# One recurrent-attention and MLP kernel: coefficients as one row spread by a product, filler transposes on TensorE, a fourth plain weight pair, and a new order table

## Chip, cores, metric

The kernel runs on one core of a Trainium2 chip. The metric is device time in microseconds (us) of one execution; smaller is better. Times of several runs are given by their median.

## What is computed

A gated linear attention over 4 x 8 sequences of 768 tokens with head size 48, and a two-layer MLP over the 3072 tokens with a rational function between its layers:

```
for t in range(S):                                  # B, H, S, D = 4, 8, 768, 48
    state = alpha[:, :, t, :, None] * state + k[:, :, t] outer v[:, :, t]
    y[:, :, t] = q[:, :, t] @ state
x = y as 3072 x 384
h = x @ w_in                                        # 384 x 2048
P = a[0] + a[1]*h + a[2]*h**2 + a[3]*h**3           # a: 4 numbers, b: 2 numbers
Q = 1 + |b[0]|*|h| + |b[1]|*h**2
out = (P / (Q + 1e-6)) @ w_out                      # 2048 x 384
```

The weights come as 64-bit floats.

## The kernel before

**Attention.** The sequences are cut into 24 chunks of 128 tokens, g = 0 to 23, with all 8 heads in one chunk. Per chunk, alpha, k and q are brought to a layout with tokens along the free axis: for the first two segments (four chunks) by TensorE transposes of loaded tiles (`turn_nat`, L515, steps `tn`) and ACT copies (L534, steps `cp`), later by DVE. Two scans on DVE give the running products from both sides (`suffix` L552, `prefix` L564, steps `suf`, `pre`); k and q are multiplied by them (L573, L576). Then TensorE transposes k (`kt`, L627), makes the scores (`s`, L594), adds to the state (`vk`, L664) and makes the chunk's y (`am`, L682). ACT and DVE copy scores out of PSUM (`se`, L615, L617) and half of q into place (`qc`, L604), GpSimd (POOL) masks them (L621). ACT writes y as x (`xh`, L712).

**MLP.** A job of layer one and two is either *wide* or *plain*. A wide job is one block of 128 hidden columns for 512 tokens: x, the weights and the rational function's result are each split into a high and a low half of a faster number format, and three products replace one (`in`: nine products of 512 columns, L792; `oh` and `ol`: nine, L811, or L805 for the last 512 tokens). A plain job is a weight pair j (256 hidden columns) for 256 tokens m, in full 32-bit floats (`plain_in` L765, `plain_out` L778; in the first jobs `in` is cut into two halves of 128 tokens). A plain product leaves two records in the trace. Plain jobs need only the whole x and the joined weights, no halves. The first `JP` = 3 pairs are plain for the first 512 tokens: jobs u = 0 to 5; the wide jobs follow, 96 jobs in all.

Between the layers each job runs through ACT (L853, L857, L860, L897), DVE (L864, L871, L874, L916) and, if wide, the split into halves (L924 or L926, L930).

**Weights.** A pair of each layer is loaded as 64-bit words (`w`, 768 KB) and made a 32-bit float: a scale step (`abs`, L358), a shift (`low`, L366), a sign step (`sign`, L370 on ACT or L372 on DVE) and `join` (L386). Pairs that are used plain are kept joined, copied by DMA later (`bring`) and split then (`hi`, `lo`); the others are split at once.

**Coefficients.** `load_coef` reads the 4 + 2 coefficients with two DMAs that repeat them over 128 partitions. Small DVE operations work out what the activations need (`unit_of`, `root_of`, `shift_of`, `sign_of`, `fits`).

**Order.** Every piece of work is a step with its engine and the steps that it comes after. A table of numbers (`ORDER`) holds the order in which all steps are written out, and with it each engine's own order; a bit in it chooses between two engines for steps that name an alternative. Each engine works its list strictly in order; loads are issued on the SP queue. At the start TensorE turns an identity matrix over 14 times (`warm`, L508) as soon as GpSimd has made it.

## Time and profile before

| | us |
|---|---|
| median of 3 runs | 511.21 (510.99 to 514.34) |
| the profiled execution | 509.78 |
| its span, from first to last instruction | 508.1 |
| TensorE busy | 489.1 (96%) |
| DVE busy | 439.3 (86%) |
| ACT busy | 400.3 (79%) |
| POOL busy | 274.3 (54%) |

By the chain that ended last, TensorE has 79% of the span and ACT 11%. In 40 slices of 12.7 us the TensorE digits are 7778899 for the first seven and 9 from then on to the last but one. The granted clock digit is 8 in the third and the fourth slice and 9 in all others.

### The profile page before, as it was taken

To read this page: it belongs to the slowest core of one execution; us is meant where nothing else is said; L and a number is where in the kernel's file an instruction comes from. 1 tells how busy PE (TensorE), PEld (TensorE's weight loads), DVE (VectorE), ACT (ScalarE), POOL (GpSimd) and SP (SyncE) were. 2 spreads that over 40 slices of the span, in tenths; PEclk is the share of its full clock that TensorE was granted. 3 is DMA by queue.
4 is the path that set the end of the run, shared out by engine and by line. 5 is a ranking of instruction groups with operands and counts; after the bars stand their busy time and mean duration, and the time that the engine had idled before them with its cause. 6 is when DMAs were issued, how large, how long until landed. Compare 5 with 4: busy or idle time off the path is not lost.

```text
span 508.1 us, 13259 instructions
## 1 busy us (share of the span) xinstructions
PE 489.1 (96%) x5062; PEld 411.1 (81%) x5062; DVE 439.3 (86%) x696; ACT 400.3 (79%) x726; POOL 274.3 (54%) x330
## 2 busy tenths in 40 slices
PE   7778899999999999999999999999999999999995
PEld 6668788787788888888888888888888888898994
DVE  4998999998998999889989989799888887877673
ACT  2898999999887778877797877788878676877572
POOL 2336567789977545647665455753646553321410
PEclk9988999999999999999999999999999999999999
DMA  7999784745643344645543545536544300321001
GB/s 199 266 280 279 193 233 96 178 99 128 154 111 86 85 92 103 106 115 117 114 97 81 122 92 114 120 82 125 98 104 79 64 22 1 57 32 17 1 0 66
DMA packets 144595, 55.98 MB, mean 110 GB/s; under 512 B 133520, under 2 KB 137104, under 8 KB 144528
## 3 DMA queue, kind: packets, MB, share of 16 engines
q1 hardware_dynamic: 143952, 54.70, 46.8%
q8 instruction: 41, 0.67, 0.6%
q10 hardware_dynamic: 576, 0.40, 0.2%
q14 instruction: 26, 0.21, 0.1%
HBM read 47.98 MB, written 4.72 MB: 104 GB/s over the span
## 4 chain that ended last, share of the span: by engine, by line
PE 79%; ACT 11%; DMA 4%; DVE 2%; issue 2%; POOL 1%; SPq 1%; ACTq 0%; DVEq 0%; POOLq 0%
PE ps L792 33%; PE ps L811 29%; PE ps L805 6%; PE ps L682 4%; PE ps L594 2%; PE ps L664 2%; ACT wi_words L370 1%; DMA wo_words<-in_moe_w_out_dram 1%; PE ps L627 1%; DMA wi_words<-in_moe_w_in_dram 1%; ACT t L860 1%; DMA coef<-in_moe_b_dram 1%; ACT qm L857 1%; ACT qm L853 1%; ACT tqk L615 1%
## 5 line engine op out<-in xcount | busy, mean ns | idle before, releaser
L792 PE MATMUL ps<-x,wi 128*128 128x512 f32 x810 | 201.8, 392 | 0.0
L792 PEld LDWEIGHTS ps<-x,wi 128*128 128x128 f32 x810 | 151.2, 188 | 31.2 <-DVE t L916 0.4
L811 PE MATMUL ps<-gh_gl,wo 128*128 128x512 f32 x666 | 167.7, 393 | 0.1
L811 PEld LDWEIGHTS ps<-gh_gl,wo 128*128 128x128 f32 x666 | 123.5, 188 | 26.5 <-POOL gh_gl L930 0.5
L930 POOL TENSOR_TENSOR gh_gl<-t,gh_gl 128x512 fp32r<-128x512 f32 x72 | 93.2, 1296 | 74.6 <-PE ps L811 20.6
L864 DVE SCALAR_TENSOR_TENSOR t<-t,mini,ps 128x512 f32<-128x512 f32 x96 | 70.8, 739 | 20.5 <-ACT t L860 14.5
L860 ACT ACTIVATE t<-ps,mini 128x512 f32<-128x512 f32 x96 | 65.7, 684 | 23.0 <-PE ps L792 10.7
L871 DVE SCALAR_TENSOR_TENSOR t<-t,mini,ps 128x512 f32<-128x512 f32 x96 | 70.6, 736 | 14.6 <-ACT ps L897 13.9
L853 ACT ACTIVATE qm<-ps 128x512 f32<-128x512 f32 x96 | 56.8, 594 | 22.4 <-PE ps L792 16.6
L897 ACT ACTIVATE ps<-qm 128x512 f32<-128x512 f32 x96 | 57.4, 601 | 21.2 <-DVE t L864 20.0
L857 ACT ACTIVATE qm<-qm,mini 128x512 f32<-128x512 f32 x96 | 69.3, 722 | 1.1
L926 POOL CAST gh_gl<-t 128x512 fp32r<-128x512 f32 x55 | 33.5, 612 | 62.8 <-DVE t L916 33.5
L916 DVE SCALAR_TENSOR_TENSOR t<-ps,t 128x512 f32<-128x512 f32 x96 | 65.7, 685 | 1.9
L874 DVE SCALAR_TENSOR_TENSOR ps<-qm,ps 128x512 f32<-128x512 f32 x96 | 65.9, 687 | 0.0
L621 POOL TENSOR_SCALAR_AFFINE_SELECT tqk<-tqk 64x512 f32<-64x512 f32 x48 | 31.5, 655 | 23.7 <-DVE tqk L617 11.4
L573 POOL TENSOR_TENSOR tqk<-tqk,tg 128x512 f32<-128x512 f32 x23 | 29.6, 1289 | 13.6 <-DVE wo_words L366 7.3
L805 PE MATMUL ps<-wo,gh_gl 128*128 128x384 f32 x180 | 34.1, 336 | 0.0
L805 PEld LDWEIGHTS ps<-wo,gh_gl 128*128 128x128 f32 x180 | 31.8, 188 | 1.3
L564 DVE TENSOR_TENSOR_SCAN fp<-ta,ps 128x528 f32<-128x528 f32 x24 | 29.9, 1244 | 1.4 <-ACT tqk L615 0.5
L552 DVE TENSOR_TENSOR_SCAN tg<-ta,ps 128x528 f32<-128x528 f32 x24 | 29.8, 1246 | 1.1 <-ACT qm L853 0.8
L576 POOL TENSOR_TENSOR tqk<-tqk,fp 128x512 f32<-128x512 f32 x19 | 24.6, 1295 | 7.2 <-DVE fp L564 4.0
L924 ACT ACTIVATE gh_gl<-t 128x512 fp32r<-128x512 f32 x35 | 21.9, 626 | 8.3 <-DVE t L916 8.2
(137 smaller groups left out, 619.4 us busy)
## 6 DMA issues: line engine op xcount, KB each, us to landing
raw_a<-in_alpha_dram SPq DMA_DIRECT2D x160, 48.0 KB, 2.1
wi_words<-in_moe_w_in_dram SPq DMA_DIRECT2D x8, 768.0 KB, 6.5
wo_words<-in_moe_w_out_dram SPq DMA_DIRECT2D x8, 768.0 KB, 6.0
sv<-in_v_dram SPq DMA_DIRECT2D x48, 96.0 KB, 2.8
wr<-in_alpha_dram SPq DMA_DIRECT2D x18, 256.0 KB, 3.0
raw_odd<-in_q_dram SPq DMA_DIRECT2D x80, 48.0 KB, 2.3
raw_qk<-in_k_dram SPq DMA_DIRECT2D x80, 48.0 KB, 2.2
raw_qk<-in_q_dram SPq DMA_DIRECT2D x80, 48.0 KB, 2.2
```

What stands on the lines that cost most here:

```text
L792: nc.tensor.matmul(h_of(u), w(key)[:, kt * FU + f % FU, :], x[:, kt, xp, :], start=(n == 0), stop=(n == len(todo) - 1),)
L805: nc.tensor.matmul(bank(T_BANKS[tt], DM), g[:, tt * P : (tt + 1) * P], w(("o", f // FU))[:, f % FU, :], start=(f == 0 and first_w), stop=( ...
L811: nc.tensor.matmul(bank(O_BANKS[dt]), w(("o", f // FU))[:, f % FU, dt * P : (dt + 1) * P], g, start=(f == 0 and first_w), stop=(f == NF - ...
L853: nc.scalar.activation(buf(s, "qm", u), h_of(u), AF.Abs)
L857: nc.scalar.activation(t, t, AF.Square, bias=shift[:, 1:2], scale=rq_reg)
L860: nc.scalar.activation(buf(s, "t1", u), h_of(u), AF.Square, bias=shift[:, 0:1], scale=rp_reg)
L864: nc.vector.scalar_tensor_tensor(t, t, rest, h_of(u), op0=ALU.add, op1=ALU.mult)
L871: nc.vector.scalar_tensor_tensor(t, t, part_of[:, 0:1], h_of(u), op0=ALU.add, op1=ALU.mult)
L874: nc.vector.scalar_tensor_tensor(h_of(u), buf(s, "qm", u), SMALL, h_of(u), op0=ALU.add, op1=ALU.mult)
L897: nc.scalar.add_instruction(mybir.InstActivation(name=nc.get_next_instruction_name(), engine=nc.scalar.engine, func=AF.Reciprocal, ins=[nc ...
L916: nc.vector.scalar_tensor_tensor(t, h_of(u), 2.0, t, op0=ALU.subtract, op1=ALU.mult, reverse0=True)
L930: eng.tensor_tensor(buf(s, "gl", u).rearrange("p a b -> p (a b)"), buf(s, "t1", u), gh, op=ALU.subtract)
```

## The change

- The coefficients are loaded into one partition (two DMAs of one row each). A DVE memset writes a row of 128 ones (`set_ones`), a TensorE product of that row with the coefficients puts them on all 128 partitions in PSUM (`coef_mm`), and a DVE copy brings them back (`coef_all`). The steps that use them come after the copy.
- Ten groups of four transposes of the identity into bank 7 (`fill`). Three may come from the point at which that bank's first user has been copied, seven after its second; the first `plain_out` comes after all of them.
- `JP` = 4: four plain pairs, jobs u = 0 to 7 (four with the first 256 tokens, four with the next), and two wide jobs fewer.
- A new order table.

```diff
--- before.py
+++ after.py
@@ -75,63 +75,64 @@
 
 
 ORDER = [
-    'c-jrt1Dhqv4nWaLDoItwwr$(CZQC}^^qHRS9^1BU+qP}n_ult@#QxR>6T`$b35+q(O=J_r#4`yE8*9{vnP|{VGLy|>v&@i*',
...
+    'c-jq>V}mBl4h1{iNjh2Ewr$(CZQHx=vokwd+qP}nwr$(E_ZOTmRdv7^V~sP34H`1>%oG#fL^E+sEEC;KGgHk5lhDL5QB7=<',
...
 ]
 
 
@@ -148,6 +149,7 @@
 }
 NNAT = 2
 WARM = 14
+FILL = (3, 7)
 WB = 2
 GB = 3
 NSC = 1
@@ -159,7 +161,7 @@
 NV = 2
 NTG = 2
 RB = 2
-JP = 3
+JP = 4
 HALF = 3
 Y_FROM = 8
 Y_AT = (4, 8, 12, 15)
@@ -236,8 +238,17 @@
     b0, b1 = bab[:, 0:1], bab[:, 1:2]
 
     def load_coef():
-        nc.scalar.dma_start(coef[:, 0:4], ca.unsqueeze(0).to_broadcast([P, 4]))
-        nc.scalar.dma_start(coef[:, 4:6], cb.unsqueeze(0).to_broadcast([P, 2]))
+        nc.scalar.dma_start(coef[0:1, 0:4], ca.unsqueeze(0))
+        nc.scalar.dma_start(coef[0:1, 4:6], cb.unsqueeze(0))
+
+    def set_ones():
+        nc.vector.memset(fp[0][0:1, 0:P], 1.0)
+
+    def coef_mm():
+        nc.tensor.matmul(bank(2)[:, P : P + 6], fp[0][0:1, 0:P], coef[0:1, :], start=True, stop=True)
+
+    def coef_all():
+        nc.vector.tensor_copy(coef, bank(2)[:, P : P + 6])
 
     a3_reg = nc.scalar.alloc_register("a3")
     b1_reg = nc.scalar.alloc_register("b1")
@@ -506,6 +517,10 @@
     def warm():
         for n in range(WARM):
             nc.tensor.transpose(bank(2, P), ident, ident)
+
+    def fill():
+        for n in range(4):
+            nc.tensor.transpose(bank(7, P), ident, ident)
 
     def turn_nat(m, nm, par):
         for a in range(NPAIR):
@@ -1097,9 +1112,12 @@
     add("coef", "ACT", 0.8, load_coef, kb=0.1)
     if WARM:
         add("warm", "PE", 0.11 * WARM, warm, (), ["ident"], lat=0.13)
-    add("sign", "DVE", 0.3, sign_of, (), ["coef"], lock=True)
+    add("ones", "DVE", 0.15, set_ones)
+    add("coef_mm", "PE", 0.1, coef_mm, (), ["coef", "ones", "warm"], lat=0.13)
+    add("coef_all", "DVE", 0.15, coef_all, (), ["coef_mm"])
+    add("sign", "DVE", 0.3, sign_of, (), ["coef_all"], lock=True)
     add("sign_to", "ACT", 0.1, sign_to, (), ["sign"])
-    add("unit", "DVE", 0.9, unit_of, (), ["coef"], lock=True)
+    add("unit", "DVE", 0.9, unit_of, (), ["coef_all"], lock=True)
     add("root", "DVE", 0.9, root_of, (), ["unit"], lock=True)
     add("shift", "DVE", 0.35, shift_of, (), ["root", "sign"], lock=True)
     add("regs", "ACT", 0.2, regs_of, (), ["root"])
@@ -1143,6 +1161,8 @@
 
     NGC = 2 * NBLK
     nat_users = [[] for _ in range(8)]
+    fills = [("fill", n) for n in range(FILL[0])]
+    late_fills = [("fill", n) for n in range(FILL[0], sum(FILL))]
     for m in range(NNAT):
         for nm in "aqk":
             add(("nat", m, nm), "SP", DMA, load_nat, (m, nm), (), kb=1.45)
@@ -1151,7 +1171,7 @@
                 before = [("cp", *x, p, cc) for x in nat_users[b] for p in (None, 0, 1) for cc in range(2)]
                 nat_users[b].append((m, nm))
                 add(("tn", m, nm, par), "PE", 0.9, turn_nat, (m, nm, par),
-                    [("nat", m, nm), ("set", nm, m), "ident", "warm"] + before + ([("nat", m, "k"), ("set", "k", m)] if nm == "q" else []), lat=0.13)
+                    [("nat", m, nm), ("set", nm, m), "ident", "warm"] + (["coef_mm"] if b == 2 else []) + (fills if b == 7 and m else []) + before + ([("nat", m, "k"), ("set", "k", m)] if nm == "q" else []), lat=0.13)
     for g in range(NGC):
         m, cc = divmod(g, 2)
         old = [(w, g - NQ) for w in ("am", "s", "kt")]
@@ -1181,6 +1201,10 @@
         add(("q", g), "POOL", 1.3, mult_q, (g,), [("pre", g)] + ready["q"], alt=("DVE", 0.69, True))
         for c in range(2):
             add(("sv", g, c), "SP", DMA, load_sv, (g, c), [("set", "v", g % NV), ("am", g - NV), ("vk", g - NV)], kb=0.9)
+    for n in range(sum(FILL)):
+        users = nat_users[7][: 1 if n < FILL[0] else 2]
+        add(("fill", n), "PE", 0.44, fill, (), [("cp", *x, p, cc) for x in users for p in (None, 0, 1) for cc in range(2)]
+            + [("fill", x) for x in range(n)][-1:] + ["warm", "ident"], lat=0.13)
     for g in range(NGC):
         near = [("cp", *x, p, cc) for b in (SCB, SCB + 1) for x in nat_users[b] for p in (None, 0, 1) for cc in range(2)]
         was = ([("xh", g - 1), ("xl", g - 1 if g > PER else -1)] if g <= Y_FROM else []) + [("km", g - 1), ("kv", g - 1), ("se", g - 1, 0), ("se", g - 1, 1)]
@@ -1286,7 +1310,7 @@
                 old += [("cp", *x, p, cc) for b in O_BANKS for x in nat_users[b] for p in (None, 0, 1) for cc in range(2)]
                 old += ["consts"] + [(x, g) for x in ("suf", "pre") for g in range(G3)]
             add(("oh", u, ff), "PE", OH[1], plain_out, (u, ff),
-                [("g", u), ("join", ("o", j)), ("oh", u, 0) if ff else ("oh", u - 1, 1)] + old, due=at + ff)
+                [("g", u), ("join", ("o", j)), ("oh", u, 0) if ff else ("oh", u - 1, 1)] + old + (late_fills if u == 0 else []), due=at + ff)
 
 
     for n in range(NG):
```

What the new table does to DVE's list is shown where the coefficients are worked out (`mini`), ahead of the first scan. Before:

```order
L273 SCALAR_TENSOR_TENSOR mini<-mini 128x1
L276 TENSOR_SCALAR mini<-mini 128x2
L279 TENSOR_SCALAR mini<-coef 128x1
L280 TENSOR_SCALAR mini<-mini 128x1
L309 SCALAR_TENSOR_TENSOR mini<-coef 128x1
L312 SCALAR_TENSOR_TENSOR mini<-mini 128x1
L315 TENSOR_SCALAR mini<-mini 128x1
L316 TENSOR_SCALAR mini<-mini 128x2
L317 TENSOR_TENSOR mini<-mini 128x2
L318 TENSOR_SCALAR mini<-mini 128x1
L319 TENSOR_SCALAR beyond<-mini 128x3
L284 TENSOR_SCALAR mini<-mini 128x2
```

And now:

```order
L284 SCALAR_TENSOR_TENSOR mini<-mini 128x1
L287 TENSOR_SCALAR mini<-mini 128x2
L295 TENSOR_SCALAR mini<-mini 128x2
L296 TENSOR_SCALAR mini<-mini 128x2
L297 TENSOR_SCALAR mini<-mini 128x2
L299 RECIPROCAL mini<-mini 128x2
```

The nine operations of `sign_of` and `fits` (L279 to L319 before) stood between `unit_of` and `root_of`; they now stand behind q of the first chunk.

The second place is TensorE's start, with what each row waits for (DMAHW are loads, Pool the identity). Before, the warm transposes (L508) are followed by the transposes of alpha:

```order
L508 MATMUL ps<-ident 128x128 [waits Pool_49]
L508 MATMUL ps<-ident 128x128 x13
L515 MATMUL ps<-ident,raw_a_77 128x128 [waits DMAHW1_49]
L515 MATMUL ps<-ident,raw_a_77 64x128
L515 MATMUL ps<-ident,raw_a_77 128x128
```

And now:

```order
L519 MATMUL ps<-ident 128x128 [waits Pool_49]
L519 MATMUL ps<-ident 128x128 x13
L248 MATMUL ps<-coef,fp_82 128x6 [waits DMAHW2_49,DMAHW0_49,DVE_49]
L530 MATMUL ps<-ident,raw_a_77 128x128 [waits DMAHW1_49]
L530 MATMUL ps<-ident,raw_a_77 64x128
```

The product (L248) stands between the two and waits for both coefficient loads and the row of ones.

The third place is TensorE's list from the second job's second half to the fourth chunk's y (L682 with tqk_85, now L697). L765 and now L780 are the first layer's plain products, L778 and L793 the second layer's. Before:

```order
L765 MATMUL ps<-x_whole,wi_words 128x128 x12
L627 MATMUL ps<-ident,tqk_85 128x112 x4
L682 MATMUL ps<-tqk_87,sv_88 32x64 x32
L594 MATMUL ps<-tqk_85 64x64 x16
L765 MATMUL ps<-x_whole,wi_words 128x128 x6
L664 MATMUL ps<-sv_89,kt_93 64x48 x16
L778 MATMUL ps<-t_95,wo_words 128x256 x6
L682 MATMUL ps<-tqk_85,sv_89 32x64 x32
L765 MATMUL ps<-x_whole,wi_words 128x256 x6
L778 MATMUL ps<-t_96,wo_words 128x256 x3
```

And now, with the fillers as L523:

```order
L523 MATMUL ps<-ident 128x128 x8
L780 MATMUL ps<-x_whole,wi_words 128x128 x12
L642 MATMUL ps<-ident,tqk_85 128x112 x4
L780 MATMUL ps<-x_whole,wi_words 128x128 x6
L523 MATMUL ps<-ident 128x128 x4
L697 MATMUL ps<-tqk_87,sv_88 32x64 x32
L523 MATMUL ps<-ident 128x128 x4
L679 MATMUL ps<-sv_89,kt_93 64x48 x16
L609 MATMUL ps<-tqk_85 64x64 x16
L793 MATMUL ps<-t_95,wo_words 128x256 x6
L780 MATMUL ps<-x_whole,wi_words 128x256 x3
L697 MATMUL ps<-tqk_85,sv_89 32x64 x32
```

The job of 256 columns ahead of the fourth chunk's y is the fourth pair with the first 256 tokens; before, the job behind that y was the first pair with the second 256.

## Rows read from the trace of the kernel before

**Rows 1.** Engines' busy time by stretch: us, busy (instructions), granted clock, DMA share, GB/s
```profile
core 0: us, PE busy (x) PEld busy (x) DVE busy (x) ACT busy (x) POOL busy (x), PEclk, DMA share, GB/s
35.20:42.00 6.80, 5.87 (x56) 5.48 (x55) 6.42 (x11) 5.25 (x11) 3.90 (x7) 0.52 0.99 265
...
16.84:54.42 37.58, 31.18 (x631) 27.19 (x625) 34.54 (x58) 35.01 (x61) 15.91 (x28) 0.91 1.01 268
57.64:499.82 442.18, 441.85 (x4317) 370.20 (x4318) 390.69 (x594) 355.87 (x653) 251.05 (x279) 1.00 0.42 93
100.00:140.00 40.00, 39.76 (x501) 31.84 (x502) 37.94 (x60) 37.61 (x69) 36.80 (x36) 1.00 0.53 125
```

**Rows 2.** Chain of waits (start, us), and DMA issues: KB each, us to landing
```profile
1.35 5.16 DMA coef<-in_moe_b_dram
...
coef<-in_moe_a_dram ACTq DMA_DIRECT2D x1, 2.0 KB, 3.2
...
wr<-tot_beyond SPq DMA_DIRECT2D x1, 0.5 KB, 2.0
```

**Rows 3.** Timeline of DVE, coefficients and first scans
```profile
6.65 0.16 DVE L265 SCALAR_TENSOR_TENSOR mini<-coef 128x2 f32<-128x2 f32 x1 [5.07 <-DMA coef<-in_moe_b_dram]
...
8.36 0.15 DVE L279 TENSOR_SCALAR mini<-coef 128x1 f32<-128x1 f32 x1
...
9.47 0.16 DVE L284 TENSOR_SCALAR mini<-mini 128x2 uint32<-128x2 uint32 x1
...
11.54 2.43 DVE L552 TENSOR_TENSOR_SCAN tg<-ta,ps 128x528 f32<-128x528 f32 x2
```

**Rows 4.** Timeline of ACT, its waits for TensorE
```profile
8.57 0.60 ACT L534 ACTIVATE ta<-ps 128x512 f32<-128x512 f32 x1 [5.24 <-PE ps L515]
...
16.94 0.86 ACT L604 ACTIVATE tqk<-tqk 64x256 f32<-64x256 f32 x2 [0.76 <-PE ps L594]
...
41.98 0.60 ACT L853 ACTIVATE qm<-ps 128x512 f32<-128x512 f32 x1 [1.43 <-PE ps L765]
```

**Rows 5.** Timeline of TensorE where it fills up
```profile
54.42 2.86 PE L765 MATMUL ps<-x_whole,wi_words 128*128 128x256 f32 x12 [1.51 <-ACT x_whole L712]
57.64 1.56 PE L778 MATMUL ps<-t,wo_words 128*128 128x256 f32 x6 [0.36 <-DVE t L916]
59.04 1.46 PE L765 MATMUL ps<-x_whole,wi_words 128*128 128x256 f32 x6
60.33 1.46 PE L778 MATMUL ps<-t,wo_words 128*128 128x256 f32 x6
```

**Rows 6.** Timeline of TensorE, start: start, us, operation [idle before <-what ended it]
```profile
1.86 3.25 PE L508 MATMUL ps<-ident 128*128 128x128 f32 x14 [1.86 <-POOL ident masks.py:199]
5.63 2.90 PE L515 MATMUL ps<-ident,raw_a 128*128 128x128 f32 x16 [0.52 <-DMA raw_a<-in_alpha_dram]
9.55 3.71 PE L515 MATMUL ps<-ident,raw_qk 128*128 128x128 f32 x32 [1.01 <-DMA raw_qk<-in_k_dram]
14.51 0.60 PE L627 MATMUL ps<-ident,tqk 112*128 112x112 f32 x4 [1.25 <-POOL tqk L573]
```

**Rows 7.** Groups of ACT, 15 to 54.4 us: count, busy us, mean ns
```profile
L370 ACT ACTIVATE wi_words<-wi_words 128x768 f16<-128x768 f32 x3 | 5.9, 1955 | 0.0
L615 ACT ACTIVATE tqk<-ps 64x512 f32<-64x512 f32 x6 | 3.5, 592 | 0.2
...
L604 ACT ACTIVATE tqk<-tqk 64x256 f32<-64x256 f32 x8 | 3.3, 416 | 1.1 <-PE ps L594 0.8 <-POOL st L634 0.2
L644 ACT ACTIVATE sv<-st 48x192 f32<-48x192 f32 x8 | 2.9, 358 | 0.1
L358 ACT ACTIVATE parts<-wi_words 128x768 f32<-128x768 f32 x3 | 2.8, 945 | 0.0
```

**Rows 8.** Chain of waits, a wide job's in and out
```profile
126.78 2.04 PE ps L792 x9
...
130.15 2.05 PE ps L811 x9
```

More of the change, by code (lines that the diff above doesn't have):

```diff
@@ L135 @@
+    'Qd8*<`6;O*;;Pq-nqLd3XgMvfs+ly4X4Zn5RkLY!Eu@7thvrm>6i;($5iP34w7C9J6Ujz$kxob&t)vySuEy5{npW#+I!&)7',
+    'w2kJ`wwhOSYd$ThrL~M!)P~wfD{B?4s-+^TX?5+beYCzd&<@&I+i4T+s7<w**3hzAOKWS825Womt2MQb_SXU0N&D#t9jKkP',
+    'c|?ndPz}*8+Epj$M4hCQwVQU=Fb&t1+DcpNARVkjbiOXop*l=^Xix2>Q#3+H>L?u@F;y`VMH-_Eb(${L={iGa>LOjI>vgkk',
+    ')Ft|#26VX2ikPiqb)4>$@w!x(>2h76b995w)p@!yVzsW(O}a(5>Nef3t8|C%jMx>iR(I=uJ*<0luO85SdQcDP5k0O)^_ZT}',
+    'lX^=32gvYnmj',
 ]
```

108 lines of the change are left out of this document (52 added, 56 removed).

## Prediction

> **What bounds the kernel now.** I read the engines' busy time by stretch first [rows 1]. From 57.64 to 499.82 us TensorE is busy 441.85 of 442.18 us: once it is full, it stays full, and the end is the moment it fills up plus the work then left. Ahead of that, from 16.84 to 54.42 us, it is busy only 31.18 of 37.58 us, while ScalarE (ACT) has 35.01 and VectorE (DVE) 34.54. So the time can come from two places only: the work that TensorE has in all, and the first 57 us, where ACT, nearly always busy, sets the pace. The timelines of the engines then show what the first 57 us wait for. DVE starts its small coefficient operations at 6.65 us, after 5.07 us of waiting for the second coefficient load, which took 5.16 us [rows 2, 3]; the first scan of attention starts at 11.54 [rows 3]. ACT waits for TensorE until 16.94, and from there on it has only one wait of size, 1.43 us before 41.98, for the first layer's TensorE work [rows 4]. That work ran while the granted clock was low: 0.52 on average from 35.2 to 42.0 us [rows 1], so nearly all at 1.2 GHz. Last, TensorE waits 1.51 us before 54.42 for the x of the fourth chunk [rows 5].
>
> **Coefficients.** The two loads become one row each, and a 128x6 product (L248) and a DVE copy (L251) spread it. No row shows a one-row load of this kind; the nearest are 2.0 us (0.5 KB) and the first coefficient load itself, 3.2 us; the second took 5.16 [rows 2]. Issued at 1.35 us, it lands between 3.4 and 6.5 us. The product stands on TensorE behind the 14 warm transposes, which end at 1.86 + 3.25 = 5.11 [rows 6]; a load of up to 3.7 us is hidden behind them. I take that (both small loads are below it). Product and copy are a few columns; with two handovers I give them 0.3 us, so DVE begins near 5.4 instead of 6.65. The nine operations of sign and fits, which stood ahead of the root from 8.36 to 9.47, move behind the first scans: 1.1 us more. DVE would be ready at 11.54 - 1.25 - 1.1 = 9.2. The first scan now waits for ACT: its chunk is the second of two copies which begin at 8.57 and take 0.6 each [rows 4], so 9.8. Gain 1.7 us; behind the scan the chain to the first scores and to ACT's start at 16.94 is the same, so ACT starts its long run at 15.2. Bounds 0 (the load is as slow as now) and 1.9. The moved operations now stand ahead of the second chunk's prefix scan (L564, L579), which so gains less than the rest, about 0.6; behind it wait the second chunk's q and its scores, which have a whole chunk's work of TensorE ahead of them. DVE's total is the same.
>
> **The filler groups.** Ten groups of four transposes. A transpose of this size takes 3.71/32 = 0.116 us [rows 6], a group 0.47, all ten 4.7 us of TensorE. Five stand between the second chunk's k transposes (L627, L642) and the first product of layer one, five among the half jobs of layer one up to the third chunk's attention product and just behind it. Their effect would be the clock: with it up, ACT's wait of 1.43 us goes (what comes late next there is nothing of size: ACT has its other inputs). The most it can give is TensorE's own lost time, 5.87 x 0.48 = 2.8 us. I take 1.4, bounds 0 and 2.8. Do transposes hold the clock up at all? The rows say so: until 14.51 us TensorE did nothing but transposes, and they went from 3.25/14 = 0.232 us to 0.116 [rows 6], the ratio of the two levels 1.2 and 2.4 GHz. The Trainium skill's page "TensorE: Matmul & The Clock Gate", section "Part 4: PE-mode transpose", says otherwise: the full clock "doesn't engage" for transposes, as they don't count as busy in the same way. By that rule the 1.4 us would stay lost. In this trace they do engage it.
>
> Whether the groups cost anything is a question of room. Between the first scores and the point at which TensorE fills, it idles 37.58 - 31.18 = 6.4 us, and would get 2.8 us from the clock: 9.2 us. Fillers (4.7) and the fourth pair's first-layer job (2.6, below) want 7.3. So the room suffices on the whole, with 2 us over; but TensorE works in order, and a group can stand ahead of a step that is ready. Bounds 0 and 4.7; I take one group's price, 0.5 us.
>
> **ACT's list.** What ACT does up to the fourth x (L712, L727) changes: it gets two more sign steps (L370, 1.96 each) and one more score copy (L615, 0.59); it loses one scale step (L358, 0.94), two half copies of q (L604, 0.42 each) and two state copies (L644, 0.36 each) [rows 7]. One more x step and one weight split less cancel. 3.92 + 0.59 - 0.94 - 0.84 - 0.72 = 2.0 us more, to be taken off ACT's gains. Bounds 0 (part of it fills ACT's small waits) and 2.0; ACT has no waits of size, so I take 1.8. DVE, the other busy one, gets no more work there.
>
> **The fourth plain pair.** Weights of block pair 3 are used plain for the first 512 tokens. It removes two wide steps, each an in and an out of nine products at 2.04 us [rows 8]: 4 x 2.04 = 8.2 us. It adds two plain jobs; half a job is three products of 256 columns, 1.29 to 1.40 us from start to start (57.64, 59.04, 60.33) [rows 5], so a job is 5.2 and two 10.4. That is 2.2 us more for TensorE, on the path since TensorE is full. It also brings work forward: job 3 now belongs to the first 256 tokens and needs no fourth x. Half of its first layer stands ahead of the fourth chunk's attention product (L697) and half right behind. When the fourth x arrives, 2.6 us are done that were to do before, and the 1.51 us hole is filled. What it costs beside that are two copies of 384 KB (`bring`) on SP's queue, since its joined words are kept and split later; they come behind the full point, where the DMA engines are busy for a share of 0.42 [rows 1].
>
> **The table.** On SP's queue the weights of pair 0 move from fifth to eleventh, behind k and q of the second segment and the weights of pair 1. The DMA engines are at their limit here (share 1.01 [rows 1]), so the order counts; but up to the fourth x both kernels load nine weight blocks, and what waits for pair 0, the first product of layer one, now has five filler groups ahead of it. I count 0.
>
> **The sum.** The fourth x, and with it the point from which TensorE is full, now 54.42: -1.7 - 1.4 + 1.8 = -1.3, at 53.1. Work left from there: +2.2 - 2.6 = -0.4. Fillers +0.5. In all -1.2 us: span 508.1 to 506.9, and the profiled execution's own 509.78 to 508.6. The median of the runs, 511.21, lies 1.43 above that execution; I put the change against the median: 511.21 - 1.2 = **510.0**.
>
> **Rivals.**
> - *The start gains more.* ACT's extra steps fill its small waits, the clock gives all 2.8, no group costs: -1.7 - 2.8 - 0.4 = -4.9, 506.3; with the start's far bound and the 0.33 us of idling behind 57.64 gone, 505.8. For it: ACT idles 2.6 us in the stretch. Against: TensorE would have to fill up 3 us earlier, with 5 us more to do before. Between 505.8 and 508.5: 0.25.
> - *Slower: the groups stand on the path.* TensorE's queue is in order; where a group stands ahead of a ready step, 0.47 us is lost each. The forecast holds one. Without any the sum is -1.7, so from the fourth on the change loses; with all ten it is -1.7 + 4.7 = +3.0, 514.2. For it: only 2 us of room is left, and in four places a group is next to first-layer products. Against: these are places where the trace shows waits. 511.2 to 514.2: 0.12.
> - *Transposes don't hold the clock*, only products do: the stretch at 0.52 [rows 1] comes again and ACT waits as before. -1.2 + 1.4 = +0.2, 511.4. Against: the halved time of a transpose with nothing but transposes ahead of it [rows 6]. 0.06. (The Trainium skill's section named above speaks for it.)
> - *The coefficient row is as late as now.* The product then blocks TensorE's queue and the first transposes start at 6.6 instead of 5.63; the 1.7 us go: -1.2 + 1.7 = +0.5, 511.7. 0.05.
> - *New waits behind the full point.* GpSimd takes over low halves and state copies from DVE and ACT (the low halves on it go from 72 to 78) and is at 36.80 of 40 us from 100 to 140 [rows 1]; if its low halves come late, TensorE waits. 1 to 6 us more than the forecast, 511 to 516.5. Against: with two wide steps less there are two low halves less to make. 0.10.
>
> **How the numbers follow.** The forecast's own range, 508.5 to 511.2, has 0.42. What a measurement can tell from no change is about 1%, 5.1 us. Faster by more than that (under 506.1) is the far end of the first rival, and terms beyond their bounds: 0.09. Slower (over 516.3) needs the last rival's far end: 0.05. The rest, 0.86, is within 1%. The range is 505.8 to 513.5, from the far end of the first rival: below it lies 0.08, above it the larger part of the last rival and the tail of the second, about 0.1.
>
> **What would show it.** Right: DVE's first scan near 9.8 us; granted clock 1.00 from 8 us to the end; the first-layer activation (L868) without a wait of over 1 us; TensorE without holes from 53 us; eight more half jobs of plain products (L780, L793) at 1.3 us each. Wrong: a wait of L248 on the coefficient load past 5.6 us; a stretch at 1.2 GHz; fillers directly behind and ahead of work with no wait between; waits of TensorE for GpSimd after 60 us.

## The result, and the profile after

The changed kernel takes 505.74 us (median of 4 runs, 505.61 to 506.45) against 511.84 us before (4 runs, 510.99 to 514.34): ratio 0.9894, 95% interval 0.9866 to 0.9921. Run again on another chip it takes 507.53 (6 runs, 505.50 to 508.76) against 511.62: 0.9905, 0.9877 to 0.9933. So it is about 1% faster: by these ratios 4.9 to 5.4 us, by the medians 6.1 and 4.1. The forecast was 1.2; the first median lies 0.06 us below the range, the second inside it. By its size this is the first rival, "the start gains more"; how much of that rival's mechanism came is told below.

| us | before | after |
|---|---|---|
| profiled execution, own time | 509.78 | 505.85 |
| its span | 508.1 | 504.1 |
| DVE's first scan | 11.54 [rows 3] | 9.52 |
| ACT's long run begins | 16.94 [rows 4] | 15.09 |
| product on the fourth x | 54.42 [rows 5] | 52.03 |

The start on DVE (timeline: start, us, operation, [idle before <-what ended it]):

```profile
5.33 0.17 DVE L251 COPY coef<-ps 128x6 f32<-128x6 f32 x1 [3.58 <-PE ps L248]
5.60 0.16 DVE L276 SCALAR_TENSOR_TENSOR mini<-coef 128x2 f32<-128x2 f32 x1
...
9.52 2.39 DVE L567 TENSOR_TENSOR_SCAN tg<-ta,ps 128x528 f32<-128x528 f32 x2
```

The small operations begin at 5.60 instead of 6.65, and the scan at 9.52 instead of 11.54 [rows 3]. On TensorE, the same stretch and the point where it fills up:

```profile
1.52 3.25 PE L519 MATMUL ps<-ident 128*128 128x128 f32 x14 [1.52 <-POOL ident masks.py:199]
4.70 0.59 PE L248 MATMUL ps<-coef,fp 1*128 1x6 f32 x2
5.22 1.98 PE L530 MATMUL ps<-ident,raw_a 128*128 128x128 f32 x16
...
14.36 0.69 PE L609 MATMUL ps<-tqk 48*64 48x64 f32 x32 [1.52 <-DVE tqk L591]
...
47.61 1.46 PE L780 MATMUL ps<-x_whole,wi_words 128*128 128x256 f32 x6
48.99 1.17 PE L697 MATMUL ps<-tqk,sv 128*32 128x64 f32 x64
50.10 1.56 PE L780 MATMUL ps<-x_whole,wi_words 128*128 128x256 f32 x6
52.03 2.86 PE L780 MATMUL ps<-x_whole,wi_words 128*128 128x256 f32 x12 [0.37 <-ACT x_whole L727]
...
495.78 2.25 PE L835 MATMUL ps<-wo,gh_gl 128*128 128x384 f32 x12
```

The coefficient product has no idle time ahead of it: the row was there when the warm transposes ended. The hole ahead of the fourth x is 0.37 us instead of 1.51 [rows 5], since the two halves of job 3 stand around the attention product, as the prediction had it. In the kernel before, the last line of this list reads

```profile
499.66 2.25 PE L820 MATMUL ps<-wo,gh_gl 128*128 128x384 f32 x12
```

so from the fourth x to the last product's end there were 447.49 us and are now 446.00. The engines by stretch (us, busy (instructions), granted clock, DMA share, GB/s):

```profile
core 0: us, PE busy (x) PEld busy (x) DVE busy (x) ACT busy (x) POOL busy (x), PEclk, DMA share, GB/s
15.09:52.03 36.94, 35.56 (x676) 31.69 (x676) 35.21 (x63) 36.25 (x59) 16.72 (x29) 0.95 0.91 244
52.03:495.60 443.57, 443.56 (x4327) 372.70 (x4328) 389.76 (x594) 353.30 (x643) 258.02 (x289) 1.00 0.43 97
...
14.00:20.00 6.00, 5.64 (x88) 4.78 (x88) 5.04 (x20) 4.84 (x8) 2.59 (x3) 0.72 1.11 312
35.00:42.00 7.00, 7.00 (x123) 6.78 (x126) 6.92 (x14) 6.95 (x11) 2.47 (x5) 1.00 1.04 286
```

Up to the fourth x, ACT now idles 0.69 us (before: 2.47 of the 37.48 us from 16.94 to 54.42), TensorE 1.38. Behind it TensorE idles 0.01 us. The stretch at 1.2 GHz from 35 us on [rows 1] is gone; a shorter one, 15.5 to 18.9 us, has come.

### The profile page after: what moved, and what is told of

It is laid out like the page before. It is cut to its first block, busy times and chain, and to the rows that moved or that the text cites. A ratio compares the mean times of both kernels' runs of the same rounds, so it can differ in the third digit from the quotient of the medians.

```text
span 504.1 us, 13375 instructions
## 1 busy us (share of the span) xinstructions
PE 492.0 (98%) x5116; PEld 416.1 (83%) x5116; DVE 436.1 (87%) x695; ACT 395.8 (79%) x712; POOL 280.6 (56%) x343
## 4 chain that ended last, share of the span: by engine, by line
PE 91%; ACT 5%; DVE 2%; issue 1%; POOL 0%; ACTq 0%; POOLq 0%; DVEq 0%
PE ps L807 36%; PE ps L826 30%; PE ps L820 6%; PE ps L697 4%; PE ps L793 4%; PE ps L609 2%; PE ps L679 2%; PE ps L780 2%; PE ps L642 2%; ACT wi_words L381 1%; PE ps L530 1%; PE ps L519 1%; ACT tqk L630 1%; ACT wr L369 0%; DVE tg L567 0%
## 5 line engine op out<-in xcount | busy, mean ns | idle before, releaser
L807 PE MATMUL ps<-x,wi 128*128 128x512 f32 x792 | 196.3, 392 | 0.0
L807 PEld LDWEIGHTS ps<-x,wi 128*128 128x128 f32 x792 | 147.9, 188 | 30.5 <-DVE x L745 0.3
L826 PE MATMUL ps<-gh_gl,wo 128*128 128x512 f32 x648 | 162.5, 393 | 0.0
L826 PEld LDWEIGHTS ps<-gh_gl,wo 128*128 128x128 f32 x648 | 120.4, 188 | 25.1
L945 POOL TENSOR_TENSOR gh_gl<-t,gh_gl 128x512 fp32r<-128x512 f32 x78 | 100.8, 1297 | 69.0 <-ACT gh_gl L939 29.4
L886 DVE SCALAR_TENSOR_TENSOR t<-t,mini,ps 128x512 f32<-128x512 f32 x96 | 70.7, 738 | 21.3 <-ACT ps L912 20.7
L941 POOL CAST gh_gl<-t 128x512 fp32r<-128x512 f32 x57 | 34.9, 613 | 70.9 <-DVE t L931 55.0
L912 ACT ACTIVATE ps<-qm 128x512 f32<-128x512 f32 x96 | 57.6, 601 | 20.8 <-DVE t L879 18.8
L588 POOL TENSOR_TENSOR tqk<-tqk,tg 128x512 f32<-128x512 f32 x22 | 28.3, 1290 | 12.7 <-DVE tg L567 6.7
L697 PEld LDWEIGHTS ps<-tqk,sv 128*32 128x32 f32 x1536 | 22.6, 110 | 5.1 <-issue 1.7
L697 PE MATMUL ps<-tqk,sv 128*32 128x64 f32 x1536 | 26.5, 221 | 0.0
```

Source lines behind the costliest of these rows:

```text
L697: nc.tensor.matmul(y[r : r + 32, o : o + CH], w[:, w0 : w0 + 32], tqk[g % NQ][:, int(j == c), a, toks(c)], start=r not in begun, stop=True ...
L807: nc.tensor.matmul(h_of(u), w(key)[:, kt * FU + f % FU, :], x[:, kt, xp, :], start=(n == 0), stop=(n == len(todo) - 1),)
L826: nc.tensor.matmul(bank(O_BANKS[dt]), w(("o", f // FU))[:, f % FU, dt * P : (dt + 1) * P], g, start=(f == 0 and first_w), stop=(f == NF - ...
L886: nc.vector.scalar_tensor_tensor(t, t, part_of[:, 0:1], h_of(u), op0=ALU.add, op1=ALU.mult)
L912: nc.scalar.add_instruction(mybir.InstActivation(name=nc.get_next_instruction_name(), engine=nc.scalar.engine, func=AF.Reciprocal, ins=[nc ...
L945: eng.tensor_tensor(buf(s, "gl", u).rearrange("p a b -> p (a b)"), buf(s, "t1", u), gh, op=ALU.subtract)
```

## The experiments

Each run's profiled execution can be read as two numbers: when the product on the fourth x begins (the *full point*), and how long the execution lasts from there (own time less full point). I give both for all, with the stretches ahead of 60 us in which the granted clock was at 1.2 GHz. "The same early clock" further down means that the early stretch at 1.2 GHz is of the same kind in both executions: none, a short one or a long one. One execution was profiled of each kernel, two of the kernel before and of the changed kernel.

| kernel | own time | at 1.2 GHz | first scan | ACT's run | full point | left |
|---|---|---|---|---|---|---|
| before | 509.78 | 34.9-41.7 | 11.54 | 16.94 | 54.42 | 455.36 |
| before, again | 509.94 | 15.6-22.5, 36.1-39.5 | 11.50 | 17.34 | 54.67 | 455.27 |
| before, row alone | 511.97 | 14.5-21.3, 35.0-38.4 | 10.84 | 16.68 | 54.02 | 457.95 |
| before, filler groups alone | 512.62 | none | 11.51 | 16.91 | 53.00 | 459.62 |
| after | 505.85 | 15.5-18.9 | 9.52 | 15.09 | 52.03 | 453.82 |
| after, again | 507.17 | 14.0-20.8 | 9.52 | 15.53 | 53.37 | 453.80 |
| after, no filler groups | 508.57 | 14.1-20.9 | 9.52 | 15.53 | 53.32 | 455.25 |
| after, eight in a group | 510.95 | 14.0-20.8 | 9.53 | 15.53 | 57.16 | 453.79 |
| after, four early groups more | 507.33 | none | 9.53 | 15.10 | 51.64 | 455.69 |
| after, broadcast loads | 508.00 | 15.1-21.9 | 10.41 | 16.41 | 54.38 | 453.62 |
| after, sign and fits ahead of root | 506.64 | none | 10.50 | 16.08 | 52.98 | 453.66 |
| after, three ACT steps twice | 508.79 | 15.2-18.6 | 9.41 | 14.98 | 54.80 | 453.99 |
| after, job 3 without layer one | 507.46 | 14.3-17.7, 51.8-55.3 | 9.53 | 15.54 | 51.90 | 455.56 |
| after, pair 0's weights fifth | 508.42 | 14.3-21.1 | 9.53 | 15.53 | 54.12 | 454.30 |

My theory after the result was that the sum's steps were right and its sizes small. The rivals: that the fillers do it, that the start does it, that the table does it.

**The two kernels again.** No edit.

> The kernel before, unchanged, to see why its median (511.84) lies 2 us above its profiled execution (509.78) while the changed kernel's runs lie within 505.6 to 506.5. Theory: its runs differ in how long TensorE's clock is low, so runs of 512 to 514 us show a mean granted clock below the 0.991 of the profiled one, by about 0.004 for each 2 us. Rival: the runs differ at the same clock, and the difference has another source (loads). Expected median 511 to 512.5.

Measured: 511.04 us (12 runs, 509.26 to 513.90), 1.0 (0.9975 to 1.0026). Its profile has two stretches at 1.2 GHz, elsewhere than in the first profile, and the full point is only 0.25 us later. So which stretches run at 1.2 GHz differs between executions of one kernel. ACT's wait of 1.43 us for the first layer [rows 4] is not there in this execution; it waits about as long 21 us earlier, for transposes in the first low stretch:

```profile
20.94 1.09 ACT L534 ACTIVATE ta<-ps 128x512 f32<-128x512 f32 x2 [1.51 <-PE ps L515]
```

In the runs a lower mean clock goes with a longer time only loosely: over the 46 runs of this kernel on this chip the correlation is -0.55, and 0.004 of clock go with 1.0 us where the theory said 2 (509.0 and 511.9 us both stand at 0.995). The clock alone does not make the spread of some 4 us.

> The changed kernel unaltered, as the reference on this chip for the others (nine kernels built from it or from the kernel before are compared). If what was seen first holds: ratio to the kernel before 0.987 to 0.992, about 505.7 us, the fourth-x layer-one product (L780) at 52.0 us, granted clock low for one stretch of 3.4 us near 15 to 19 us at most, and runs within about 1 us of one another. If the narrow spread of its first four runs was luck, the runs spread over 4 us as those of the kernel before do, and the ratio comes nearer to that of the kernel without filler groups (0.994).

Measured: 507.53 us, 0.9905 (0.9877 to 0.9933). The narrow spread of the first four runs was luck. This profile shows what the early clock is worth. The first k transposes begin at 12.24 us and the first scores at 14.36 in both executions, but in this one the scores run at 1.2 GHz,

```profile
14.36 1.13 PE L609 MATMUL ps<-tqk 48*64 48x64 f32 x32 [1.52 <-DVE mini L290]
15.43 1.97 PE L530 MATMUL ps<-ident,raw_second 128*128 128x128 f32 x8
```

1.13 us instead of 0.69. ACT's run begins 0.44 us later, the full point 1.34 later (53.37), and the own time is 1.32 longer; what is left behind the full point is equal to 0.02 us. The full point carries all of the difference.

**The coefficient row.** Taken out of the changed kernel (the loads broadcast again, order as changed), and put alone into the kernel before:

```
-nc.scalar.dma_start(coef[0:1, 0:4], ca.unsqueeze(0))            # and cb
+nc.scalar.dma_start(coef[:, 0:4], ca.unsqueeze(0).to_broadcast([P, 4]))
-memset, product and copy of L245, L248, L251
```

> The changed kernel with the coefficients loaded over 128 partitions again, without product and copy; the order stays. Theory: DVE's small operations begin at 6.65 us instead of 5.60, the first scan at 10.5 to 10.6 instead of 9.52, ACT's long run 1 us later, and since ACT paces the kernel up to the point where TensorE is full, the time rises by 0.8 to 1.1: 506.5 to 506.8. Rival (the start is taken up by the loads' pace further on): 505.7, with the fourth x at 52.0 as now.

Measured: 508.66 us (12 runs, 506.49 to 511.10), 0.9956 (0.9933 to 0.9979). Against the same early clock, first scan and ACT's run are 0.89 and 0.88 us later and the full point 1.01 (54.38 against 53.37), the rest equal to 0.2 us. In the profiles the row is worth 1 us in this order. By the ratios of the runs it is 2.6 us, with intervals that just touch; where more than 1 us would come from, no profile shows.

> The kernel before with one part of the change alone: coefficients as one row, product on TensorE, copy on DVE; order, pairs and loads otherwise as before (no filler groups, three plain pairs, sign and fits ahead of the root). Theory 1 (the row is worth what the start gains, and the start carries to the full point): DVE's small operations from 5.6 instead of 6.65, first scan at 10.4 to 10.5 instead of 11.54, ACT's long run from 15.9 instead of 16.94, fourth-x product at 53.4 instead of 54.42, time 1.0 us lower: ratio 0.997 to 0.999. Theory 2 (the broadcast loads of 128 small pieces each also disturb the loads behind them, and so make the spread of 4 to 5 us of every kernel that has them): the median falls by 2 to 3 us, ratio 0.994 to 0.996, and the runs lie within 2 us. Theory 3 (ACT's list sets the full point whatever the start): first scan earlier, fourth-x product still at 54.2 to 54.5, ratio 1.000.

Measured: 511.95 us (12 runs, 510.10 to 512.41), 0.9995 (0.9976 to 1.0014): no change that the runs can tell. The first scan comes 0.70 us earlier, the full point 0.40, and then TensorE waits for the function between the layers, where the kernel before waited 0.36 us at one place [rows 5]:

```profile
57.25 1.56 PE L785 MATMUL ps<-t,wo_words 128*128 128x256 f32 x6 [0.37 <-DVE t L923]
75.09 2.86 PE L785 MATMUL ps<-t,wo_words 128*128 128x256 f32 x12 [0.73 <-DVE t L923]
80.50 1.43 PE L799 MATMUL ps<-x,wi 128*128 128x512 f32 x5 [0.47 <-DVE t L923]
```

In this execution the start's gain is given back behind the full point, and loads stand ahead of the two later waits: DVE waits 0.64 us for in weights at 71.56 and 1.05 us for q at 78.50. The in weights' load is issued on SP's queue at 63.67 us, in the kernel before at 62.66, where DVE did not wait for it. Why it is issued later was not traced. This profile is also the one near the median of its runs (511.97), unlike that of the kernel before. Theory 2, that the broadcast loads as such cost 2 to 3 us, falls in the old order. Its other half, that they make the spread, does not: the standard deviation of these twelve runs is 0.72 us, of the 20 of the kernel before beside them 1.26, and over all runs, each taken about the mean of its kernel and chip, 0.88 for the kernels with the row (74 runs) and 1.30 for those with the broadcast (111 runs). What would make it, no profile shows.

**The filler groups.** Taken out of the changed kernel, put alone into the kernel before (seven groups, ahead of the third chunk's k transposes, scores and state product and the fourth's scores and state product), and doubled:

```
-        for n in range(4):
-            nc.tensor.transpose(bank(7, P), ident, ident)
+        pass                     # or: for n in range(8)
```

> The changed kernel with the ten filler groups left out of TensorE's list, all else the same. Theory (the groups stand where TensorE waits, and keep its clock up): the granted clock falls to 1.2 GHz in a further stretch between 20 and 50 us, ACT waits there for layer one, and the time is 506.7 to 507.5 against 505.7. Rival 1 (they stand on the path): 504 to 505.2, at the same clock. Rival 2 (the new order alone keeps TensorE busy enough): 505.7, and the clock as in the changed kernel.

Measured: 507.63 us (11 runs, 506.84 to 508.84), 0.9940 (0.9917 to 0.9962). Without any filler group the clock is at 2.4 GHz from 20.9 us on, and the full point is at 53.32, against 53.37 of the same early clock with all ten. Up to the full point they neither hold the clock up here nor cost anything. From 32 to 36 us, ahead of the old low stretch, TensorE is busy 3.63 of 4.00 us in this kernel without fillers (first line), and 2.54 in the kernel before (second line):

```profile
32.00:36.00 4.00, 3.63 (x34) 3.38 (x38) 3.90 (x7) 4.00 (x7) 1.28 (x1) 1.00 0.70 217
32.00:36.00 4.00, 2.54 (x42) 2.22 (x41) 3.50 (x6) 3.88 (x7) 0.00 (x0) 0.86 0.85 231
```

What fills it is layer-one work, which the new order puts there. All three executions of the old order without fillers have a stretch at 1.2 GHz between 34.9 and 41.7 us, and none of the ten of the changed order has one between 22 and 51. That the order does it is read from the trace, and from row, moved operations, fillers, job 3's first layer and pair 0's load having each been taken out without such a stretch coming back. The new order was not run alone, without the fourth pair. Behind the full point this execution lasts 1.45 us longer; 0.7 of that is seen as TensorE's idling between 80 and 150 us. Whether the groups have a part in that, the runs do not settle: the medians differ by 0.1 us, the ratios by 0.0035 to 0.0046, at the edge of their intervals.

> The kernel before with seven groups of four transposes put in front of the steps for which TensorE waited between 31 and 48 us, nothing else changed. Theory: the clock stays at 2.4 GHz between 30 and 45 us, ACT's wait of 1.43 us goes, and the time falls by 1.0 to 1.6 us against the kernel before at its usual clock. Rival 1 (transposes don't hold the clock): no change in clock, time the same or up to 2 us longer. Rival 2 (the groups delay ready steps): the clock holds, but the time is the same.

Measured: 509.58 us (12 runs, 508.07 to 512.88), 0.9979 (0.9953 to 1.0006), not told apart from no change. In the old order fillers do what the prediction says of them: there is no stretch at 1.2 GHz ahead of the full point, which comes at 53.00 instead of 54.42, 1.42 us earlier. But this execution, one of the longest of its twelve, then loses more than it won,

```profile
57.36 1.56 PE L780 MATMUL ps<-t,wo_words 128*128 128x256 f32 x6 [1.51 <-DVE t L918]
76.53 4.49 PE L780 MATMUL ps<-t,wo_words 128*128 128x256 f32 x12 [2.12 <-DVE t L918]
```

where the waits of DVE name a weight load:

```profile
DVE wi_words L364 <- DMA wi_words<-in_moe_w_in_dram: 3.0, 2, 2.0
```

(us in total, times, longest.) The load behind the longer of the two waits is issued on SP's queue at 65.02 us and lands 7.96 us later; in the kernel before (second line) the same load is issued at 62.66:

```profile
65.02 7.96 DMA wi_words<-in_moe_w_in_dram
62.66 0.43 SPq L346 DMA_DIRECT2D wi_words<-in_moe_w_in_dram  x1
```

So the load comes later although the full point is earlier; why was not traced. The second line of the timeline also runs at 1.2 GHz, 4.49 us instead of 2.86, after 2.12 us of idling.

> The changed kernel with eight transposes in each filler group instead of four: 40 more, 0.116 us each, 4.7 us more of TensorE's time before it is full. Theory 1 (the groups stand in holes where TensorE waits for ACT, DVE or loads, but the changed kernel has only about 1.4 us of idling left from 15.1 to 52.0 us): 1.4 of the 4.7 us are hidden, the fourth-x product comes at 55.3 instead of 52.0, and 3.3 us more in all, ratio to the kernel before about 0.996. Theory 2 (what TensorE does in front of the fourth x is paced by ACT and DVE, and holes open as soon as work ahead is later): 0 to 1 us more. Theory 3 (every group is on the path): 4.7 us more, ratio 0.9985.

Measured: 510.06 us (9 runs, 509.07 to 511.35), 0.9962 (0.9940 to 0.9984), 2.5 us over the changed kernel on the same chip. In the profiles the full point goes from 53.37 to 57.16: 3.79 of the added 40 x 0.116 = 4.64 us are on the path, 0.85 are hidden. Theory 1 holds.

```profile
15.53:57.16 41.63, 40.72 (x716) 36.82 (x716) 35.23 (x61) 37.02 (x59) 16.83 (x29) 0.94 0.87 228
```

Now TensorE is busy 40.72 of the 41.63 us between ACT's start and the full point, and ACT idles 4.61: the bound has changed hands. The ten groups of the change had used the room up but for 0.85 us.

> The changed kernel with four more groups of four transposes (1.9 us of TensorE) early: two ahead of the first chunk's k transposes, two ahead of its scores, where TensorE waits for DVE's first scan and for ACT. Theory 1 (the low stretch of the clock at 15.5 to 18.9 us follows from the idling ahead of it, and costs the start some time): no stretch at 1.2 GHz after 5 us, the first scores not later, fourth-x product 0.5 to 1.5 us earlier, time 0.5 to 1.5 us less. Theory 2 (in that stretch TensorE is not what is waited for): clock full, time the same within 0.3 us. Theory 3 (the groups delay the first transposes and scores): 0.5 to 1.9 us more.

```
+    def early_fill():
+        for n in range(4):
+            nc.tensor.transpose(bank(2, P), ident, ident)
     two groups ahead of the first chunk's kt, two ahead of its s
```

Measured: 506.28 us (6 runs, 505.20 to 508.01), 0.9881 (0.9855 to 0.9907). The early stretch at 1.2 GHz is gone:

```profile
8.00:14.00 6.00, 5.96 (x56) 5.72 (x53) 5.52 (x15) 3.80 (x7) 2.58 (x3) 1.00 1.01 281
14.00:20.00 6.00, 5.00 (x124) 4.24 (x128) 5.04 (x20) 4.83 (x9) 2.59 (x3) 1.00 1.07 316
```

and the full point is the earliest of all, 51.64: 0.39 us ahead of the first profile, 1.73 of the second. This execution loses 1.9 us behind it, of which 1.1 are seen as TensorE's idling (0.41 us for DVE's t at 96.28, 0.35 for POOL's masked scores at 107.51). By the medians it is 1.2 us better than the changed kernel beside it, but the intervals overlap: a candidate, not shown to be faster. Nor does one execution show that the groups took the early stretch away: the kernel with sign and fits ahead of the root (below) has none either, without them.

**Who sets the full point.** Three scale steps of ACT done twice:

```
-            eng.activation(o, x, AF.Copy, scale=2.0 ** -112)
+            for _ in range(2 if key in (("i", 3), ("o", 0), ("i", 4)) else 1):
+                eng.activation(o, x, AF.Copy, scale=2.0 ** -112)
```

> The changed kernel with three ACT steps done twice ahead of the full point (the scale steps L369 of the in weights of pairs 3 and 4 and of the out weights of pair 0, 0.93 us each). Theory 1 (ACT sets the full point, being busy 36.25 of 36.94 us up to it): fourth-x product 2.4 to 2.8 us later, time 2.4 to 2.8 more, ratio to the kernel before about 0.9955. Theory 2 (ACT's list overlaps itself or its slack hides it): 0 to 0.5 us more. In between would mean that ACT and TensorE take turns.

Measured: 508.76 us (9 runs, 508.18 to 509.64), 0.9945 (0.9928 to 0.9962). Full point 54.80, 2.77 us later than in the execution of like early clock, own time 2.94 longer:

```profile
14.98:54.80 39.82, 35.65 (x676) 31.73 (x676) 35.52 (x63) 39.07 (x62) 16.78 (x29) 0.96 0.85 234
```

ACT's busy time grew by 39.07 - 36.25 = 2.82 us, and the full point moved by as much to 0.05. ACT's list sets the pace of this stretch.

> The changed kernel without the layer-one products of plain job 3 (the fourth pair on the first 256 tokens: two half jobs of six products, 1.25 to 1.3 us each, one on either side of the fourth chunk's attention product); what they would have computed is left out, all else as it is. Theory 1 (the two half jobs stand in holes that would be there without them, since the full point is set by ACT's list): fourth-x product at the same time to within 0.3 us, TensorE idling some 2 us more ahead of it, time the same within 0.5 us; so the fourth pair has brought 2.6 us of work forward for nothing. Rival (TensorE paces this stretch): fourth-x product 1.3 to 2.6 us earlier, time as much lower.

```
         m, j = jobs[u][1:]
+        if u == 3:
+            return
         for kt in range(KT):
```

Measured: 508.68 us (8 runs, 506.91 to 510.72), 0.9942 (0.9915 to 0.9969): with two half jobs less to do it is not faster. The full point is at 51.90, against 52.03 in the first execution of the changed kernel. The early clocks differ, but from 21 us on this execution runs 0.1 us ahead of that one (k transposes L642 at 21.02 against 21.11), so the two halves stand in holes, as forecast. What was not expected by either theory is the next product:

```profile
48.38 1.68 PE L697 MATMUL ps<-tqk,sv 128*32 128x64 f32 x64 [0.72 <-POOL tqk L636]
51.90 4.49 PE L782 MATMUL ps<-x_whole,wi_words 128*128 128x256 f32 x12 [1.84 <-ACT x_whole L727]
```

```profile
51.00:55.40 4.40, 3.50 (x9) 2.84 (x10) 4.40 (x8) 4.38 (x8) 1.36 (x4) 0.61 1.06 294
```

Behind the open hole the twelve products take 4.49 us instead of 2.86, with a granted clock of 0.61 on average over 51.0 to 55.4 us. That is 1.63 of the 1.74 us by which this execution is longer behind its full point than the changed kernel. So in this execution the work left out of the hole is paid for by the clock behind it. The filler run of the old order shows the same behind 2.12 us of idling; behind the 1.41 to 1.51 us ahead of the fourth x in the four executions of the old order the twelve products took 2.86 us.

**The start's other half, and the table.** The nine DVE operations of sign and fits moved back ahead of the root; and pair 0's in weights moved back from eleventh to fifth on SP's queue (both by the order table alone):

> The changed kernel with the nine DVE operations of sign and fits back ahead of the root, where they stood before; all else as it is. Theory 1 (DVE's small operations are the chain to the first scan, and the start carries to the full point): first scan 1.0 us later, 10.5 instead of 9.52, ACT's long run from 16.0 instead of 15.1 to 15.5, fourth-x product 0.7 to 1.0 later, time 0.7 to 1.0 more. Theory 2 (ACT makes up for a later start out of its small waits, as the kernel with the row alone seems to say: first scan 0.7 earlier, ACT's run 0.26, full point 0.4, time nothing): first scan 1.0 later, fourth-x product 0.5 later or less, time the same within 0.5 us.

Measured: 506.77 us (5 runs, 506.49 to 508.29), 0.9913 (0.9880 to 0.9946). First scan 10.50, 0.98 later; ACT's run 16.08, 0.99 later. This execution has no early stretch at 1.2 GHz, although TensorE idles ahead of the first scores as long as in the changed kernel:

```profile
15.35 0.69 PE L606 MATMUL ps<-tqk 48*64 48x64 f32 x32 [1.52 <-DVE tqk L588]
```

Its full point, 52.98, lies 0.95 behind the first profile's, which has a short low stretch, and 1.34 behind that of the kernel with early groups, which has none. So in the profiles the moved operations are worth 1 us or a little more; the medians (507.53 for the changed kernel on another chip) do not show it.

> The changed kernel with one load moved back on SP's queue: the in weights of pair 0 (768 KB) fifth instead of eleventh, behind the first segment's alpha, k and q and ahead of the second segment's k, q and alpha, the weights of pair 1 and v. Theory 1 (as the prediction put it: the loads' order counts for nothing): time the same within 0.5 us. Theory 2 (the DMA engines are at their limit up to 56 us, so 768 KB at about 300 GB/s put off all that stands behind by 2.5 us): k, q and v land 2.5 us later, the first chunks' state product and the second chunk's scores wait for them, fourth-x product 1 to 2.5 us later and the time as much more. Theory 3 (what waits for pair 0 is late in the changed kernel): 0.5 to 1.5 us less.

Measured: 507.05 us (4 runs, 506.79 to 508.42), 0.9904 (0.9867 to 0.9940): as the changed kernel. In its profile, its longest execution, the full point is 0.75 us later than at the same early clock, and DVE waits for a load of out weights:

```profile
DVE wo_words L374 <- DMA wo_words<-in_moe_w_out_dram: 0.7, 1, 0.7
```

So the place of this load is worth 0.75 us at the full point in that execution, and nothing that the runs can tell.

## Why the prediction was right and wrong

The frame was right: TensorE is full from a point on, that point is set by ACT's start and ACT's list, and a little less work is left behind it. The direction came out of it. The sizes, term by term, once from the first profiles of the two kernels (509.78 and 505.85 us) and once from the second (509.94 and 507.17):

| term | forecast | first profiles | second profiles |
|---|---|---|---|
| ACT's start | -1.7 | -1.85 (16.94 to 15.09) | -1.81 (17.34 to 15.53) |
| ACT's waits gone | -1.4 | -1.78 (2.47 to 0.69) | -1.01 (2.42 to 1.41) |
| ACT's list | +1.8 | +1.24 (35.01 to 36.25) | +1.52 (34.91 to 36.43) |
| full point, from these three | -1.3 | -2.39 | -1.30 |
| fillers | +0.5 | | +0.05 (53.32 against 53.37) |
| work left | -0.4 | -1.49 (447.49 to 446.00) | -1.53 (447.56 to 446.03) |
| sum | -1.2 | -3.9 | -2.8 |

(The measured sums leave the fillers' 0.05 out, since it is already in the rows above it. They agree with the profiled executions' own differences, 3.93 and 2.77.)

The full point was forecast at 53.1 and came at 52.03 and 53.37: it depends on where the low stretches of the clock fall. What was too small in both is the work left. The first rival, which the size points to, asked for -1.7 - 2.8 = -4.5 at the full point with ACT's list costing nothing; -2.4 and -1.3 came, and ACT's list did cost. The rest of the size comes from the work left and from the step to the median (last point below), so that the time lies near that rival's far end is in part luck.

- **Coefficients and start: the size right, two steps wrong.** The row was hidden behind the warm transposes, DVE began at 5.60 (forecast 5.4), the scan at 9.52 (9.8), ACT at 15.09 (15.2). For the 0.3 us of product, copy and handovers I had no row; they took 0.83, from the end of the warm transposes at 1.52 + 3.25 = 4.77 to 5.60, which shows little because TensorE began 0.34 us earlier than before (1.52 against 1.86 [rows 6]). And "the first scan now waits for ACT" did not come: ACT's two copies ran from 7.23 to 8.32 (in the kernel before only the first began at 8.57, the second at 12.02), and the scan follows DVE's own operations, the last of which begins at 9.44. Each of the two parts carries about 1 us to the full point in the changed order: 1.01 for the row, 0.95 to 1.34 for the moved operations. But the same row alone in the old order brought nothing that the runs can tell: in its profile the full point is 0.40 us earlier, and waits behind it take that back.
- **The clock: size near, cause wrong.** The step "with it up, ACT's wait of 1.43 us goes" came true, but I gave it to the filler groups. The kernel without them has the clock up from 20.9 us on as well and the same full point. The order of the layer-one work is what is left to have done it; its half jobs fill 32 to 36 us. The wait itself was one execution's: in the second profile of the kernel before, with the low stretch elsewhere, ACT waits 1.51 us at another place, and the changed kernel's second profile still has 0.81 of that. Fillers alone in the old order do give the 1.4 us (54.42 to 53.00): the term was right for a kernel in which only they change. What I failed to do was to ask what the other edits do to the same hole.
- **That transposes hold the clock** held: in the kernel with four early groups more, TensorE does nothing but transposes from 8 to 14 us, nearly without a pause, and the granted clock is 1.00 there; and the fillers alone in the old order leave no low stretch ahead of the full point, where the three other executions of that order have one. The Trainium skill's page "TensorE: Matmul & The Clock Gate", section "Part 4: PE-mode transpose", says that the full clock does not engage for them; the runs here show otherwise. The row that I had argued from is weaker: the granted clock reads 1.00 from 0 to 5 us in the profile of the kernel before, so the slow first transposes (0.232 us) show in their durations only.
- **The signs.** Two signs of being wrong came: a stretch at 1.2 GHz (15.5 to 18.9 us), and fillers between pieces of work with no wait (from 35 to 42 us TensorE is busy 7.00 of 7.00 us with three groups in it). The first matters: between the two profiles of the changed kernel a longer low stretch moved the full point by 1.34 us. The second cost nothing up to the full point, as the kernel without fillers shows.
- **ACT's list: mis-sized.** I added durations. ACT's instructions overlap in the trace, so that the sign step is 1.93 us long but the next instruction begins 1.67 us after it:

```profile
17.28 1.93 ACT L381 ACTIVATE wi_words<-wi_words 128x768 f16<-128x768 f32 x1
18.95 0.81 ACT L659 ACTIVATE sv<-st 48x192 f32<-48x192 f32 x2
```

  Two of them are 0.6 us less than I counted, which is most of the way from +1.8 to +1.24. What ACT does counts in full, as the three doubled steps show (2.82 us more busy, 2.77 us later).
- **The fillers' price: too high by half a microsecond**, but the sum of the room was good. "The room suffices on the whole, with 2 us over": doubling them showed 0.85 us over.
- **The fourth pair: the step "brings work forward" was right** (leaving job 3's first layer out leaves the full point where it is), and so was "the hole is filled". Mis-sized was what is left, by 1.1 us: 0.69 of it is idling behind the full point that I left in the sum (0.70 us before, 0.36 of them at 57.64 [rows 5], 0.01 after), and the work itself came out at -0.80 instead of -0.4. I did not trace that last 0.4 further. The term also has a side that I did not see: with the hole open, the one execution profiled lost 1.63 us more by the clock.
- **The table counted as 0**: the one load that I named moves the full point by 0.75 us in the one execution profiled, the time not measurably. But the table also holds the order of the layer-one work, which I did not price. The rival of new waits behind the full point, whose range should have ended at 510.0 + 6 = 516.0 and not at 516.5, did not come: TensorE idles 0.01 us there, though GpSimd is as busy from 100 to 140 us (36.23 of 40, before 36.80 [rows 1]).
- **From the execution to the median: wrong by about 1 us.** I put the change of one execution against the median of the runs, as if what lies between them were the same in both. The kernel before was profiled in executions of 509.78 and 509.94 us, 2.1 and 1.1 below the medians of the runs beside them (511.84, 511.04); the changed kernel's, 505.85 and 507.17, lie at theirs to 0.4 us. So the runs' difference, 4.9 to 5.4 by the ratios, is larger than that of the profiles, 3.9 for the first two and 2.8 for the second. Two kernels with the old order were profiled in executions of 512.0 and 512.6 us, and there TensorE waits 1.6 and 3.6 us behind the full point for the function between the layers, with loads issued later than in the kernel before. That the kernel before loses its extra microsecond in the same way is possible but not shown, since none of its longer executions was profiled; and the changed order had such waits too, in two of its variants (0.7 and 1.1 us). This part of the 4.9 to 5.4 us stays open.

## To carry to other kernels

Where one engine is full from a point on, read every execution as two numbers, the full point and the time left. Here the second was 453.6 to 454.0 us in six of the ten executions of the changed order, whatever the first was, so in those an edit's effect of 1 us on the full point could be read, which the medians did not resolve. It takes executions with the same early clock, since the clock alone moved the full point by 1.3 us. A hole in TensorE's work was filled here by real work brought forward, and with that work in place the fillers added nothing: ask what a filler is worth with the other edits in place. And follow an early start to the next things that TensorE needs: in the old order, in the two executions profiled, what was won at the front was waited away behind the full point, where loads came later.

## What the runs showed of the hardware

- Less work did not take less time: with two half jobs (some 2.6 us) left out, the granted clock fell after 1.84 us of idling, and twelve products of 256 columns took 4.49 us instead of 2.86.
- Executions of one kernel differ in which stretches run at 1.2 GHz (before: 34.9 to 41.7 us in one, 15.6 to 22.5 and 36.1 to 39.5 in another; after: 15.5 to 18.9 and 14.0 to 20.8), and with equal starts this alone moved the time by 1.3 us.
- From 8 to 14 us TensorE did nothing but transposes, in the kernel with early groups, and the granted clock was 1.00.
- Two coefficient loads as one row were there by 4.70 us, where the broadcast over 128 partitions landed at 6.5 [rows 2].
